# Spectral mixing and FFN in one kernel: loads reordered, scheduler weights replaced, work moved between engines

## The chip, the cores and the metric

The kernel runs on one core of a Trainium2 chip. The metric is device time in microseconds (us), the median of several executions. A core has a TensorE (matmul), a VectorE, a ScalarE, a GpSimd and a SyncE; in the profile they are PE (with PEld for its weight loads), DVE, ACT, POOL and SP. All transfers between DRAM and the core's memory (SBUF) are issued here by SyncE and run on 16 DMA engines. TensorE writes to PSUM, from where VectorE or ScalarE must copy results to SBUF.

## The reference

```python
# x: 1 x 2048 x 512, w_r, w_i: 2048 x 257, w1: 512 x 1792, w2: 1792 x 512, all bf16
def _layernorm(x, axis=-1, eps=1e-5):
    m = jnp.mean(x, axis=axis, keepdims=True)
    v = jnp.var(x, axis=axis, keepdims=True)
    return (x - m) / jnp.sqrt(v + eps)

def _A_ref(x, w_r, w_i):                       # global spectral filter
    X = rfft2(x.astype(float32), axes=(-2, -1))
    X = X * (w_r + 1j * w_i)
    return irfft2(X, s=(S, D), axes=(-2, -1)).astype(bfloat16)

def _B_ref(x, w1, b1, w2, b2):                 # dense FFN with squared ReLU
    h = einsum("bsd,df->bsf", x, w1) + b1
    r = where(h > 0, h, 0)
    return einsum("bsf,fd->bsd", r * r, w2) + b2

h  = x + _A_ref(_layernorm(x), A_w_r, A_w_i)
h2 = h + _B_ref(_layernorm(h), B_w1, B_b1, B_w2, B_b2)
```

## The kernel before

Both transforms are done as matmuls with tables of sines that the kernel computes itself. The 2048 rows lie as 128 partitions x 16 groups g. A forward first level along the rows (tables KR, one per group, scaled by 1/std of the row) is followed by a transform along the columns (GF) and a second level along the rows (EF), in eight pairs `pr` of frequencies. The products with W, their sums and folds follow on VectorE, then the inverse (EI, GI, KI). For a pair other than 0 the mirrored frequency is needed too: it is made either on VectorE ("X<-AB") or by more matmuls (`BY_PE`). Groups 0 and 1 are finished on a short path of their own; the others are finished one by one while the FFN of earlier groups runs on TensorE. The FFN runs in five chunks of 2, 3, 4, 4 and 3 groups.

No engine reorders its own instructions. Their order is fixed when the program is built, by a list scheduler: each `add` names an engine (or several to choose from), an assumed duration, what it reads and writes, a priority and, for transfers, an assumed time to landing (`lag`). The scheduler simulates these and emits each engine's instructions in that order.

```python
    def add(self, eng, w, fn, reads=(), writes=(), prio=0.0, alloc=None, at=0.0, shared=False, lag=0.0,
            uses=(), order=()):
        ways = dict(zip(eng, w)) if isinstance(eng, tuple) else {eng: w}
# ... (cut: choice of the task that can start first, buffers, the lock between DVE and POOL)

    CH = ((0, 2), (2, 4), (4, 8), (8, 12), (12, 16))
    LAND = (3.4, 3.7, 6.0, 6.3, 6.6)
    for c, (a, b) in enumerate(CH):
        add("SP", 0.45, lambda a=a, b=b: sy.dma_start(xs[:, a:b, :], xv[:, a:b, :]),          # L254
            writes=[("x", g) for g in range(a, b)], prio=c, at=0.7, lag=LAND[c])
    for i in range(2):                       # W: natural half, then the mirrored half through DRAM
        add("SP", 0.5, lambda i=i: sy.dma_start(W[i][:, 0:9, :], wv[i][:, 0:9, 1:L + 1]), writes=[("Wn", i)],
            prio=5 + i, lag=9.0)
        add("SP", 0.5, lambda i=i: sy.dma_start(wx[i][:].rearrange("k j l -> j k l"),
                                                wv[i].rearrange("k j l -> j k l")[9:16, ::-1, 1:L + 1]),
            writes=[("wx", i)], prio=7 + i, lag=10.0)
        add("SP", 0.5, lambda i=i: sy.dma_start(W[i][:, 9:16, :], wx[i][:]), reads=[("wx", i)], writes=[("Wr", i)],
            prio=20 + i, lag=4.0)                                                             # L265
# ... (cut: index tables on POOL; KF from kft, the sine of fiK)
    act(1.2, lambda: sc.activation(fiE[0][:], idxE[:], ACT.Identity, scale=cE[:]), 0.3, ...)
    act(1.2, lambda: sc.activation(fiE[1][:], idxE[:], ACT.Identity, scale=cE[:], bias=qtc[:]), 0.4, ...)
    # then Sin of fiE[i] -> EF[:, i], and EF[:, 2] = -EF[:, 0]; EI[:, i] are DMA transposes of EF[:, i]

    ON_ACT = (4, 7, 10, 13)                  # groups whose statistics ScalarE takes
    BATCH = ((0, 2), (2, 4), (4, 8), (8, 12), (12, 14), (14, 16))
        # per batch, on POOL: rs1 = var + eps; rs1 = rs1 ** -0.5
            add(("DVE", "POOL"), (0.2, 0.41), kr, reads=[("rs", bi), "KF"], writes=[("KR", g)], prio=z - 5, shared=True)
        # first level (L391, L393): 8 matmuls of 256 columns for two groups; copies of it to Bt (L399)
    # FFN loads: W1, W2, b1b, b2b
        add("SP", 0.5, lambda d=d, s=s: sy.dma_start(d, s), writes=[("FW", k)], prio=30 + k, lag=15.0, reads=["EF0"])

    BY_PE = (3, 5, 7)
    act(1.07, lambda: sin_of(flat(GI[:]), lo(flat(fiI[:]))), 27.0, reads=["fiI"], writes=["GI0"])
    act(1.4, lambda: sc.activation(junk[:, 0:1], eps[:], ACT.Sqrt), 28.0, reads=["GI0", "eps"], writes=["sqrt"])
    dve(0.15, lambda: ve.tensor_copy(b1f[:], b1b[:]), 200.0, reads=[("FW", 2)], writes=["b1f"], shared=True)
    # pairs pr = 0..7: p2 (L449) -> U (L458) -> p3 (L475-514) -> AB (L521) -> X (L528, not BY_PE)
        for i in range(2):                   # L538; mirrored half Wr for every pair but 0
            k = ("mA", "mB")[i]
            dve(0.61, lambda pr=pr, i=i: prod(pr, i), z, reads=[("X", pr), ("Wn", i)] + [("Wr", i)] * (pr > 0),
                writes=[(k, pr)], alloc=(k, (k, pr)))
    # Z (L546), fold M (L557, L559), p4 (L579), T2 (L588)
            act(0.25, lambda: et(7, 0, 2), z, reads=[("p4", 7)], writes=["T2a"])   # groups 0, 1 need T2a alone
            dve(0.6, lambda: et(7, 9, 16, ve.tensor_copy), z + 3, reads=[("p4", 7)], writes=["T2"])
            act(0.59, lambda: et(7, 2, 9), z + 9, reads=[("p4", 7)], writes=["T2"])
# ... (cut: short path of groups 0 and 1)

    CHUNKS = ((0, 2), (2, 5), (5, 9), (9, 13), (13, 16))
            if c > 0:                        # preparation of group g
                # s5: 4 matmuls (L678-681) -> p5;  od: half of p5 copied by ScalarE (L686)
                # lv1: q = p5 +- od, FP32, 2 on VectorE (L691)
                # spec: 4 columns of R (L700); lv2, k = 0..3: R <- q (L708), 127 columns each:
                    ve.tensor_tensor(o, x, y, (ALU.add, ALU.subtract, ALU.subtract, ALU.add)[k])
                # s6: one matmul of 512 columns, KI x R (L714)
                # hs = p6 + x (L716); square sum of hs - mean on ScalarE (L597)
            pool(1.17, lambda g=g: gp.tensor_tensor(hb[:, g, :], hs[:, g, :], b2b[:], ALU.add), late + 80 + g,
                 reads=[("hs", g), ("FW", 3), ("UT", c)], writes=[("hb", g)])                # L719
        # per chunk: rs2 = sqrt(...), reciprocal; u = (hs + nm1) * rs2 on VectorE for every group (L756);
        # two halves of transposes (L765) for the whole chunk; UT copied by ScalarE and VectorE (L771)
        for f in range(NF):                  # NF = 14
            # up: 4 matmuls of 128 n columns -> ph (L784); relu with bias b1f on ScalarE -> rl (L791)
            # sqr: act = rl * rl on VectorE (L797)
        # down: 14 matmuls of 512 columns per group -> po (L806); ot = po + hb on VectorE (L814); store
```

Of the kernel before, what the change touches and what calls it, by code (L numbers as in the profile page):

```python
# [15 lines left out]
P = 128  # L16
# [17 lines left out]
class Plan:  # L34
# [6 lines left out]
    def __init__(self, caps):  # L41
        self.tasks, self.caps, self.use, self.made = [], caps, {}, {}
        self.free = {e: 0.0 for e in self.HOP}
        self.held = {t: [] for t in caps}
        self.lock = {"DVE": 0.0, "POOL": 0.0}
        self.log = []

    def add(self, eng, w, fn, reads=(), writes=(), prio=0.0, alloc=None, at=0.0, shared=False, lag=0.0,
            uses=(), order=()):
        ways = dict(zip(eng, w)) if isinstance(eng, tuple) else {eng: w}  # L50
        t = dict(eng=None, ways=ways, w=0.0, fn=fn, reads=list(reads), writes=list(writes), prio=prio, alloc=alloc, at=at,
# [36 lines left out]
    def run(self):  # L88
# [7 lines left out]
        while any(left.values()):  # L96
# [28 lines left out]
            if t["alloc"]:  # L125
                tag, key = t["alloc"]
                _, old = self.slot(tag)
                if old is not None:
                    self.held[tag].remove(old)
                self.held[tag].append(key)  # L130
            t["end"] = r + t["w"]
# [8 lines left out]
            t["fn"](*([e] if len(t["ways"]) > 1 else []))  # L140
# [3 lines left out]
def kernel(  # L144
# [42 lines left out]
    rs2 = persist.tile([P, G], FP32, name="rs2")  # L187
    eps = persist.tile([P, 1], FP32, name="eps")
    mv2 = persist.tile([P, 2], FP32, name="mv2")
    junk = persist.tile([P, D], BF16, name="junk")  # L190

# [7 lines left out]
    CN = fwd.tile([P, 3, P], BF16, name="CN")  # L199
# [6 lines left out]
    fz = fwd.tile([P, 512], BF16, name="fz")  # L206
# [23 lines left out]
                 "ph": 3, "po": 2, "pp": 3, "rl": 6, "act": 2, "od": 2, "q": 2, "R": 3, "u2": 2, "UT": 2, "ot": 3})  # L230
    add = plan.add

    def mm_tile(key, dt=FP32):
        T[key] = ps.tile([P, 4096 // mybir.dt.size(dt)], dt, tag="mm", name="m_" + str(key[0]))
        return T[key]
# [16 lines left out]
    LAND = (3.4, 3.7, 6.0, 6.3, 6.6)  # L252
# [6 lines left out]
    for i in range(2):  # L259
        add("SP", 0.5, lambda i=i: sy.dma_start(W[i][:, 0:9, :], wv[i][:, 0:9, 1:L + 1]), writes=[("Wn", i)],  # L260
            prio=5 + i, lag=9.0)
        add("SP", 0.5, lambda i=i: sy.dma_start(wx[i][:].rearrange("k j l -> j k l"),
                                                wv[i].rearrange("k j l -> j k l")[9:16, ::-1, 1:L + 1]),
            writes=[("wx", i)], prio=7 + i, lag=10.0)
# [41 lines left out]
    dve(0.15, lambda: ve.memset(eps[:], EPS), 0.0, writes=["eps"])  # L306
# [10 lines left out]
    for t in range(2):  # L317
        for r in range(2):
            dve(0.34, lambda t=t, r=r: ve.tensor_scalar(fiG[:, t, r, :], idxG[:], pF[:, 3 + t:4 + t],
                                                        float((QT, HT)[r]), ALU.mult, ALU.add),  # L320
                0.6, reads=["pF", "idxG"], writes=[("fiG", t)], shared=True)
    dve(0.33, lambda: ve.scalar_tensor_tensor(
# [4 lines left out]
    act(1.2, lambda: sc.activation(fiE[0][:], idxE[:], ACT.Identity, scale=cE[:]), 0.3, reads=["idxE", "cE"],  # L327
        writes=["fiE0"])
    act(1.2, lambda: sc.activation(fiE[1][:], idxE[:], ACT.Identity, scale=cE[:], bias=qtc[:]), 0.4,
        reads=["idxE", "cE", "qtc"], writes=["fiE1"])  # L330
    act(0.2, lambda: sin_of(flat(kft[:]), lo(fiK[:])), 0.1, reads=["fiK"], writes=["kft"])
    for t in range(2):
        act(0.6, lambda t=t: sin_of(flat(GF[:, t]), lo(flat(fiG[:, t]))), 0.6 + t / 10, reads=[("fiG", t)],
            writes=["GF"])
    for i in range(2):
        act(1.1, lambda i=i: sin_of(flat(EF[:, i]), lo(fiE[i][:])), 0.5 + i / 10, reads=[f"fiE{i}"],
            writes=[f"EF{i}"])
    dve(0.46, lambda: ve.tensor_scalar(EF[:, 2], EF[:, 0], -1.0, None, ALU.mult), 3.0, reads=["EF0"],
# [12 lines left out]
    ON_ACT = (4, 7, 10, 13)  # L351
    BATCH = ((0, 2), (2, 4), (4, 8), (8, 12), (12, 14), (14, 16))
    RT = float(1.0 / np.sqrt(D))
    for bi, (a, b) in enumerate(BATCH):
        z = 10 * bi + 10
        for g in range(a, b):
            if g in ON_ACT:
                act(0.67, lambda g=g: sc.activation(junk[:], xs[:, g, :], ACT.Identity, scale=-RT / D,
                                                    accum_out=nmr[:, g:g + 1]), z - 30, reads=[("x", g)],
                    writes=[("sm", g)])  # L360
                act(0.67, lambda g=g: sc.activation(junk[:], xs[:, g, :], ACT.Square, scale=RT, bias=nmr[:, g:g + 1],
                                                    accum_out=mv1[:, g, 1:2]), z - 30, reads=[("x", g), ("sm", g), "mv1z"],
                    writes=[("mv", g)])
            else:
                def bn(g=g):
# [6 lines left out]
        pool(0.3, lambda a=a, b=b: gp.tensor_scalar(rs1[:, a:b], mv1[:, a:b, 1], EPS, None, ALU.add), z - 1,  # L372
             reads=mvs, writes=[("va", bi)])
        pool(0.4 + 0.16 * (b - a), lambda a=a, b=b: gp.tensor_tensor(rs1[:, a:b], rs1[:, a:b], mhalf[:, 0:b - a],
                                                                   ALU.pow), z - 1, reads=[("va", bi), "mhalf"],
             writes=[("rs", bi)])
        for g in range(a, b):
            def kr(e, g=g):
                (ve if e == "DVE" else gp).tensor_scalar(flat(KR[:, g]), flat(KF[:]), rs1[:, g:g + 1], None, ALU.mult)  # L379
            add(("DVE", "POOL"), (0.2, 0.41), kr, reads=[("rs", bi), "KF"], writes=[("KR", g)], prio=z - 5, shared=True)  # L380
# [37 lines left out]
    BY_PE = (3, 5, 7)  # L418
    dve(0.25, lambda: ve.tensor_scalar(CN[:], EF[:, 1, 3:8:2], -1.0, None, ALU.mult), 75.0, reads=["EF1"],
# [6 lines left out]
    act(1.07, lambda: sin_of(flat(GI[:]), lo(flat(fiI[:]))), 27.0, reads=["fiI"], writes=["GI0"])  # L426
    act(1.4, lambda: sc.activation(junk[:, 0:1], eps[:], ACT.Sqrt), 28.0, reads=["GI0", "eps"], writes=["sqrt"])
    for e in range(2):
        dve(0.3, lambda e=e: ve.tensor_scalar(GI[:, e::2], GI[:, e::2], hsc[:] if e else WSC, None, ALU.mult), 180.0,
# [3 lines left out]
    dve(0.15, lambda: ve.tensor_scalar(nm1[:, ON_ACT[0]::3], nmr[:, ON_ACT[0]::3], 1.0 / RT, None, ALU.mult), 190.0,  # L433
# [6 lines left out]
    for pr in range(8):  # L440
# [18 lines left out]
        if pr < 2:  # L459
            add(("ACT", "DVE"), (0.59, 0.67), lambda e, pr=pr, eu=eu: eu(pr, 0, 1, COPY[e]), reads=[("p2", pr, 0)],  # L460
                writes=[("U", pr), ("U", pr, 0)], uses=[("p2", pr)], alloc=("U", ("U", pr)), prio=z + 2)
            add(("ACT", "DVE"), (0.59, 0.67), lambda e, pr=pr, eu=eu: eu(pr, 1, 2, COPY[e], False),
                reads=[("p2", pr, 1)], order=[("U", pr, 0)], writes=[("U", pr), ("U", pr, 1)], uses=[("p2", pr)],
                prio=z + 2)
        else:
            act(0.93, eu, z + 2, reads=[("p2", pr)], writes=[("U", pr)], alloc=("U", ("U", pr)))
# [124 lines left out]
        else:  # L591
            act(0.25, lambda: et(7, 0, 2), z, reads=[("p4", 7)], writes=["T2a"])
            dve(0.6, lambda: et(7, 9, 16, ve.tensor_copy), z + 3, reads=[("p4", 7)], writes=["T2"])
            act(0.59, lambda: et(7, 2, 9), z + 9, reads=[("p4", 7)], writes=["T2"])
# [62 lines left out]

    CHUNKS = ((0, 2), (2, 5), (5, 9), (9, 13), (13, 16))
# [6 lines left out]
    def per(n, tab_):  # L665
        return tab_[n - 1]

    for c, (a, b) in enumerate(CHUNKS):
# [3 lines left out]
        for g in range(a, b):  # L672
            z = late + g
            if c > 0:
# [7 lines left out]
                add("PE", 0.26, s5, reads=["T2", "T2a", "GI"] + [("UT", 0)] * (g > 2), writes=[("p5", g)], prio=early + 5, alloc=("pp", ("p5", g)))  # L682
# [4 lines left out]
                act(0.37, od, z, reads=[("p5", g), ("UT", 0)], writes=[("od", g)], alloc=("od", ("od", g)))  # L687

                def lv1(g=g, i=0):
                    q = buf(ffn, ("q", g), "q", [P, 2, 2, P], FP32, 2) if i == 0 else T["q", g]  # L690
                    ve.tensor_tensor(q[:, i], T["p5", g][:, 0:256].rearrange("p (a c) -> p a c", a=2),  # L691
                                     T["od", g][:, ::-1, :], (ALU.add, ALU.subtract)[i])
                for i in range(2):
                    dve(0.35, lambda g=g, i=i: lv1(g, i), z, reads=[("p5", g), ("od", g)],
                        order=[("qh", g)] * i,
                        writes=[("q", g), ("qh", g)] if i == 0 else [("q", g)], alloc=("q", ("q", g)) if i == 0 else None)

                def spec(g=g):
                    R = buf(ffn, ("R", g), "R", [P, 512], BF16, 3)
                    ve.tensor_copy(R[:].rearrange("p (a b c) -> p a b c", a=2, b=2)[:, :, ::-1, 0],  # L700
                                   T["q", g][:, :, :, 0])
                dve(0.14, spec, z, reads=[("q", g)], writes=[("R", g), ("Rh", g)], alloc=("R", ("R", g)))

                def lv2(g=g, k=0):
# [145 lines left out]
```

## Time and profile before

| | |
|---|---|
| median of 3 runs | 200.49 us (199.92 to 201.56) |
| span of the profiled execution | 198.2 us, mean granted TensorE clock 0.919 |
| PE busy | 163.4 us, 82% |
| DVE busy | 131.3 us, 66% |
| ACT busy | 108.6 us, 55% |
| POOL busy | 41.7 us, 21% |
| DMA, all queues | 12.13 MB, of it 5 to 9 tenths of the engines busy in the first 40 us |

In the profile "L708" is line 708 of the kernel before. Durations are those of single instructions unless a count (x4) stands behind; neighbouring instructions of an engine may overlap by some tens of nanoseconds. A matmul's own duration contains its pipeline, so for the pace of many of them the distance between starts is taken. The granted clock is the share of full speed that TensorE was given.

### The profile page before, as it was taken

The page shows a single profiled execution, that of the slowest core. Times are in us where ns is not written, and L with a number is a line of the kernel's source. Part 1 is how long each engine was busy: PE and PEld are TensorE (multiplying, and loading weights), DVE is VectorE, ACT ScalarE, POOL GpSimd, SP SyncE. Part 2 cuts the span into 40 slices and gives each one's busy share as a digit, 9 for nine tenths or more (in the row PEclk, how much of TensorE's full clock was granted, in tenths as well). Part 3 has the DMA queues.
Part 4 walks back from the last instruction along what each step waited for, and adds up shares of the span by engine and source line. Part 5 has one row for each costly group of instructions (what it writes and reads, how often), then busy time and mean ns, then how long its engine had stood idle before and what let it go on. Part 6 is the DMA issues. An engine that isn't in the chain of part 4 may idle for free.

```text
span 198.2 us, 2693 instructions
## 1 busy us (share of the span) xinstructions
PE 163.4 (82%) x932; PEld 90.7 (46%) x932; DVE 131.3 (66%) x344; ACT 108.6 (55%) x187; POOL 41.7 (21%) x64
## 2 busy tenths in 40 slices
PE   7545865599983758999399897998999999999992
PEld 2223543376761426853265453453454444456540
DVE  5496261659999366899999999999722543135321
ACT  6996673199884143873378723778410772029500
POOL 7389760000000022132343204203200000000000
PEclk9978589699999585899879999999999999999998
DMA  5978999600000000000000000100010000110001
GB/s 132 371 254 191 353 252 238 206 0 0 5 0 0 0 0 2 3 0 28 26 0 3 0 26 26 31 2 0 0 53 30 26 0 0 53 49 8 0 29 50
DMA packets 15595, 12.13 MB, mean 61 GB/s; under 512 B 6110, under 2 KB 14174, under 8 KB 15582
## 3 DMA queue, kind: packets, MB, share of 16 engines
q1 hardware_dynamic: 15582, 11.97, 19.9%
q8 instruction: 7, 0.11, 0.3%
q14 instruction: 6, 0.05, 0.1%
HBM read 8.92 MB, written 3.01 MB: 60 GB/s over the span
## 4 chain that ended last, share of the span: by engine, by line
PE 39%; DVE 20%; ACT 1%; POOL 1%; issue 0%; DVEq 0%
PE po L806 20%; PE ph L784 16%; DVE act L797 5%; DVE R L708 5%; DVE hs L716 3%; DVE q L691 2%; DVE ot L814 1%; ACT rl L791 1%; PE pp L765 1%; DVE u L732 1%; PE pp L714 1%; POOL hb L719 1%; DVE R L700 1%; DVE UT L771 1%; DVE u L756 1%
## 5 line engine op out<-in xcount | busy, mean ns | idle before, releaser
L791 ACT ACTIVATE rl<-ph,b1f 128x384 bf16<-128x384 f32 (+2 forms) x70 | 41.3, 601 | 30.2 <-PE ph L784 29.0
L784 PE MATMUL ph<-UT,W 128*128 128x384 bf16 (+2 forms) x280 | 53.7, 347 | 0.0
L806 PE MATMUL po<-W,act 128*128 128x512 bf16 x224 | 50.7, 379 | 0.0
L719 POOL TENSOR_TENSOR hb<-hs,b2b 128x512 f32<-128x512 bf16 x16 | 20.2, 1267 | 93.4 <-DVE hs L716 48.2
L797 DVE TENSOR_TENSOR act<-rl 128x384 bf16<-128x384 bf16 (+2 forms) x70 | 30.6, 441 | 13.0 <-ACT rl L791 12.6
L784 PEld LDWEIGHTS <-W 128*128 128x128 bf16 x280 | 28.2, 102 | 21.0 <-issue 0.3
L806 PEld LDWEIGHTS <-act 128*128 128x128 bf16 x224 | 21.6, 98 | 26.2 <-issue 1.9
L814 DVE TENSOR_TENSOR ot<-po,hb 128x512 bf16<-128x512 f32 x16 | 11.0, 689 | 20.9 <-PE po L806 20.7
L391 PE MATMUL m_p<-KR,xs 128*128 128x256 bf16 x32 | 11.2, 360 | 8.4 <-POOL KR L379 7.9
L708 DVE TENSOR_TENSOR R<-q 128x127 bf16<-128x127 f32 x56 | 16.9, 339 | 0.0
L597 ACT ACTIVATE junk<-hs,nm 128x512 bf16<-128x512 bf16 x14 | 10.0, 717 | 8.2 <-DVE hs L716 8.2
L449 PE MATMUL m_p<-GF,Bt 128*128 128x256 bf16 x64 | 9.2, 299 | 4.8 <-DVE U L458 3.4
L458 ACT CAST U<-m_p 128x1024 bf16<-128x1024 f32 (+1 forms) x8 | 8.9, 1174 | 6.7 <-PE m_p L449 4.8
L579 PE MATMUL m_p<-EI,M 128*128 128x256 bf16 x56 | 8.6, 294 | 3.8 <-DVE M L557 3.7
L393 PE MATMUL m_p<-KR,xs 128*128 128x256 bf16 x32 | 11.2, 364 | 0.0
L588 ACT CAST T<-m_p 128x1024 bf16<-128x1024 f32 (+2 forms) x9 | 7.9, 886 | 6.0 <-DVE T L588 3.2
L691 DVE TENSOR_TENSOR q<-pp,od 128x256 f32<-128x256 f32 x28 | 10.6, 409 | 0.0
L449 PEld LDWEIGHTS <-Bt 128*128 128x128 bf16 x64 | 6.6, 106 | 6.7 <-issue 3.6
L379 POOL TENSOR_SCALAR KR<-KF,rs 128x256 bf16<-128x256 bf16 x10 | 9.4, 952 | 0.6
L716 DVE TENSOR_TENSOR hs<-pp,xs 128x512 bf16<-128x512 f32 x14 | 9.5, 679 | 0.0
L686 ACT COPY od<-pp 128x256 f32<-128x256 f32 x14 | 5.2, 369 | 7.7 <-DVE q L691 5.2
L399 ACT CAST Bt<-m_p 128x1024 bf16<-128x1024 f32 (+1 forms) x7 | 6.2, 887 | 5.2 <-PE m_p L393 3.7
(162 smaller groups left out, 210.9 us busy)
## 6 DMA issues: line engine op xcount, KB each, us to landing
W<-in_B_w_dram SPq DMA_DIRECT2D x2, 1792.0 KB, 8.4
out_dram<-ot SPq DMA_DIRECT2D x16, 128.0 KB, 1.8
xs<-in_A_x_dram SPq DMA_DIRECT2D x3, 512.0 KB, 6.5
W<-wx SPq DMA_DIRECT2D x2, 448.0 KB, 4.4
W<-in_A_w_r_dram SPq DMA_DIRECT2D x1, 576.0 KB
W<-in_A_w_i_dram SPq DMA_DIRECT2D x1, 576.0 KB, 6.4
xs<-in_A_x_dram SPq DMA_DIRECT2D x2, 256.0 KB, 5.8
wx<-in_A_w_r_dram SPq DMA_DIRECT2D x1, 448.0 KB
```

Of the source, the lines that this page charges most:

```text
L391: mm(o, lhsT=xs[:, g, P * t:P * t + P], rhs=KR[:, g, 0].unsqueeze(1).to_broadcast([P, 2, P]), start=True, stop=False)
L393: mm(o, lhsT=xs[:, g, 256 + P * t:256 + P * t + P], rhs=KR[:, g], start=False, stop=True)
L449: mm(puv[:, q, e, :], lhsT=Bt[:, 2 * t + 1 - e, 2 * pr + q, :], rhs=gfv[:, t, :, e, :], start=(t == 0), stop=(t == 1))
L691: ve.tensor_tensor(q[:, i], T["p5", g][:, 0:256].rearrange("p (a c) -> p a c", a=2), T["od", g][:, ::-1, :], (ALU.add, ALU.subtract)[i])
L708: ve.tensor_tensor(o, x, y, (ALU.add, ALU.subtract, ALU.subtract, ALU.add)[k])
L716: dve(0.67, lambda g=g: ve.tensor_tensor(hs[:, g, :], T["p6", g][:], xs[:, g, :], ALU.add), z, reads=[("p6", g)], writes=[("hs", g)])
L719: pool(1.17, lambda g=g: gp.tensor_tensor(hb[:, g, :], hs[:, g, :], b2b[:], ALU.add), late + 80 + g, reads=[("hs", g), ("FW", 3), ("UT", c ...
L784: mm(p[:, 0:P * n], lhsT=W1[:, d, bass.ts(f, P)], rhs=T["UT", c][:, d, 0:P * n], start=(d == 0), stop=(d == ND - 1))
L791: sc.activation(r[:, 0:P * n], T["ph", c, f][:, 0:P * n], ACT.Relu, bias=b1f[:, f:f + 1], scale=1.0)
L797: ve.tensor_tensor(t[:, f, 0:P * n], r[:, 0:P * n], r[:, 0:P * n], ALU.mult)
L806: mm(p[:], lhsT=T["act", c][:, f, bass.ts(i, P)], rhs=W2[:, f, :], start=(f == 0), stop=(f == NF - 1))
L814: ve.tensor_tensor(o[:], T["po", g][:], hb[:, g, :], ALU.add)
```

## The change

Five things are bundled. (1) x is issued ahead of W, a dummy Sin loads the sine table at once, and one argument table moves to POOL. (2) The scheduler's assumed durations and landing times are replaced by ones read from a trace; matmuls on zeros are put into gaps of TensorE that the scheduler foresees; which groups ScalarE takes, the batches, and the pairs done `BY_PE` change. (3) hb, the addition of the second bias, moves from GpSimd to VectorE. (4) The preparation of groups for the FFN is spread: group i of chunk c may start after the matmuls for f = 2i of chunk c-1; chunks 1 and 2 are normalised and transposed group by group, on either engine. (5) For groups 2 to 8 the second column level, four additions and a copy on VectorE, is done by nine matmuls that accumulate in PSUM.

```diff
+            self.gap = r - self.free[e]
+    def warm(p):
+        for _ in range(min(24, int((plan.gap - 0.2) / 0.08))):
+            mm(p[:, 0:P], lhsT=fz[:, 0:P], rhs=fz[:, 0:P], start=True, stop=True)
     def mm_tile(key, dt=FP32):
+        warm(T[key])
-    LAND = (3.4, 3.7, 6.0, 6.3, 6.6)
+    LAND = (3.2, 3.4, 4.2, 4.8, 5.6)
@@ natural half of W, mirrored half to DRAM
-            prio=5 + i, lag=9.0)
+            prio=5 + i, at=1.0, lag=7.0)
-            writes=[("wx", i)], prio=7 + i, lag=10.0)
+            writes=[("wx", i)], prio=7 + i, at=1.0, lag=8.0)
+    act(1.5, lambda: sc.activation(junk[:, 0:1], eps[:], ACT.Sin), -100.0, reads=["eps"], writes=["sinset"])
-    act(1.2, lambda: sc.activation(fiE[1][:], idxE[:], ACT.Identity, scale=cE[:], bias=qtc[:]), 0.4,
+    pool(1.9, lambda: gp.tensor_scalar(fiE[1][:], idxE[:], cE[:], float(QT), ALU.mult, ALU.add), 1.9,
-    ... EF[:, 2] = -EF[:, 0] ... 3.0, reads=["EF0"],
+    ... EF[:, 2] = -EF[:, 0] ... 79.0, reads=["EF0"],
-    ON_ACT = (4, 7, 10, 13)
-    BATCH = ((0, 2), (2, 4), (4, 8), (8, 12), (12, 14), (14, 16))
+    ON_ACT = (5, 7, 9, 11)
+    SQ = 6
+    BATCH = ((0, 4), (4, 8), (8, 12), (12, 14), (14, 16))
-        pool(0.3, ... rs1 = var + eps
+        dve(0.13, ... rs1 = var + eps
-            add(("DVE", "POOL"), (0.2, 0.41), kr, ...
+            add(("DVE", "ACT"), (0.28, 0.43), kr, ...
-    BY_PE = (3, 5, 7)
+    BY_PE = (4, 5, 6, 7)
-    act(1.07, ... GI ..., 27.0, reads=["fiI"], writes=["GI0"])
-    act(1.4, ... ACT.Sqrt), 28.0, reads=["GI0", "eps"], writes=["sqrt"])
+    act(1.07, ... GI ..., 27.0, reads=["fiI", ("KR", 13)], writes=["GI0"])
+    act(1.4, ... ACT.Sqrt), 0.0, reads=["GI0", "eps", ("p4", SQ)], writes=["sqrt"])
+            act(0.32, lambda: et(7, 0, 2), z, reads=[("p4", 7)], writes=["T2a"])
+            add(("ACT", "DVE"), (0.5, 0.55), lambda e: et(7, 2, 8, COPY[e]), prio=z + 30, reads=[("p4", 7)], order=["T2a"], writes=["T2"])
+            add(("ACT", "DVE"), (0.58, 0.62), lambda e: et(7, 8, 16, COPY[e]), prio=z + 60, reads=[("p4", 7)], order=["T2a"], writes=["T2"])
@@ FFN
+    def gate(c, i, n):
+        return [("ph", c - 1, 2 * i)] if c > 1 else []
+    BY_PE2 = (2, 3, 4, 5, 6, 7, 8)
+    ONE = (1, 2)
-                add("PE", 0.26, s5, reads=["T2", "T2a", "GI"] + [("UT", 0)] * (g > 2), ...
+                add("PE", 0.26, s5, reads=["T2", "T2a", "GI"] + gate(c, g - a, n), ...
@@ s6 of groups in BY_PE2 (q is bf16 there)
+                    for k in range(4):
+                        o = p[:, 128 * k + 1:128 * k + 128]
+                        for b in range(2):
+                            v = q[:, k // 2, b, :0:-1] if k % 2 == 0 else q[:, k // 2, b, 1:]
+                            mm(o, lhsT=KI[:, 1 if b == 1 and k in (1, 2) else 0], rhs=v, start=(k == 0 and b == 0), stop=False)
+                    mm(p[:].rearrange("p (a b c) -> p a b c", a=2, b=2)[:, :, ::-1, 0], lhsT=KI[:, 0], rhs=q[:, :, :, 0],
+                       start=False, stop=True)
-            pool(1.17, ... hb ..., late + 80 + g, reads=[("hs", g), ("FW", 3), ("UT", c)], ...
+            dve(0.62, ... hb ..., late + 180 + g, reads=[("hs", g), ("FW", 3), ("ph", c, 4)], writes=[("hb", g)], shared=True)
@@ chunks 1 and 2 by group (ONE): sqrt, reciprocal, nr2 = nm1 * rs2, un on DVE or ACT, transposes, UT on ACT or DVE
+                dve(0.16, ... ve.tensor_tensor(nr2[:, p0:p1], nm1[:, p0:p1], rs2[:, p0:p1], ALU.mult), z, ...
+                add(("DVE", "ACT"), (0.42, 0.72), un, ...
+            parts = [(g - a, g - a + 1, 0, 4) for g in range(a, b)] if c in ONE else [(0, n, 0, 2), (0, n, 2, 4)]
@@ relu: on DVE too in chunk 0
+            add(("ACT", "DVE") if c == 0 else ("ACT",), (0.28 + 0.085 * n, 0.1 + 0.14 * n)[:2 if c == 0 else 1], relu, prio=z, ...
```

Cut from the diff: most replaced durations, names and buffer counts. Lines with "..." are shortened.

## The prediction

> **What bounds the kernel now.** I read the chain of waits first, then busy time by stage, then the order of time of the queues at the seams. The chain, in order of time, reaches back only to 73.5 us, but its last third is plain:
>
> ```profile
> 152.21 12.09 PE ph L784 x56
> 164.29 12.09 PE po L806 x56
> 176.38 9.10 PE ph L784 x56
> 185.48 9.08 PE po L806 x42
> 194.56 0.04 DVEq L814
> ```
>
> From 139 us TensorE runs without a hole: 56 matmuls of 512 columns in 12.09 us are 0.216 us each, 56 of 384 columns 0.1625 us each. Nothing is to be had there but fewer matmuls. The busy time of stretches that I cut at the seams (engine columns PE, PEld, DVE, ACT, POOL; then the granted clock):
>
> ```profile
> 42.50:65.00 22.50, 17.57 (x135) 12.49 (x132) 21.43 (x48) 17.79 (x18) 0.00 (x0) 0.97 0.00 1
> 65.00:77.20 12.20, 7.91 (x44) 4.79 (x44) 6.21 (x14) 4.04 (x11) 2.31 (x2) 0.64 0.00 1
> 77.20:99.30 22.10, 18.10 (x125) 11.45 (x123) 20.17 (x65) 11.71 (x29) 5.44 (x4) 0.89 0.04 13
> 99.30:120.60 21.30, 20.48 (x129) 11.37 (x128) 21.18 (x62) 13.19 (x29) 5.42 (x4) 0.96 0.03 11
> 120.60:139.40 18.80, 16.73 (x95) 8.03 (x93) 18.29 (x48) 14.31 (x28) 5.77 (x5) 1.00 0.04 11
> 139.40:194.60 55.20, 55.15 (x279) 26.51 (x276) 20.89 (x46) 19.91 (x33) 1.27 (x1) 1.00 0.07 24
> ```
>
> From 42.5 to 65 (the spectral products) VectorE is 95% busy, and so it is from 77 to 139 (FFN while the next token groups are prepared), where TensorE has its holes. Before 42.5 neither is the bound. The timeline there (SyncE issues transfers; the bracket is the idle time before an instruction and what ended it):
>
> ```profile
> 1.89 4.01 SPq L254 DMA_DIRECT2D xs<-in_A_x_dram  x5
> ...
> 8.30 0.69 DVE L367 BATCH_NORM_STATS2 st<-xs 128x6 f32<-128x512 bf16 x1 [0.89 <-DMA xs<-in_A_x_dram]
> ...
> 27.14 6.61 SPq L416 DMA_DIRECT2D b2b<-in_B_b_dram  x1
> 33.80 1.90 SPq L265 DMA_DIRECT2D W<-wx  x2
> ...
> 35.91 0.17 DVE L435 CAST b1f<-b1b 128x14 f32<-128x14 bf16 x1 [3.98 <-DMA b1b<-in_B_b_dram]
> ...
> 42.53 0.69 DVE L538 TENSOR_TENSOR mA<-X,W 128x1024 bf16<-128x1024 bf16 x1
> ```
>
> Two limits lie on top of each other. The first level (L391, L393) starts at 12.5 and ends at 28.7, because x lands late and GpSimd makes most of the scaled KR tables (ten of 0.95 us). Behind it stands the load of the mirrored half of W, issued last: 33.80 plus 4.4 us to landing gives 38.2, the second 39.7. Every product from pair 1 on needs it (42.53 is the first). The DMA engines show 9, 7, 8, 9, 9, 9, 6 tenths from 5 to 40 us: moving everything there costs about 33 us of the first 40.
>
> **What the Trainium skill says.** "DMA: Bandwidth & Descriptors", section "Issuing engines are not separate DMA queues": transfers all end on the same 16 DMA engines. So reordering loads changes who waits, not the sum; the tenths above agree. "SBUF — State Buffer", section "SBUF: two separate sides": the port pair shared by VectorE and GpSimd is an exclusive lock for a whole instruction. The trace agrees: L708 takes 0.28 us elsewhere and 1.24 us at 103.14, beside GpSimd's hb of 1.20 us at 103.03. "ScalarE: Activation LUTs", section "What ACT_TABLE_LOAD costs": about 1283 ns; the trace has three at 1283 ns, and after the one for Sin none before Identity and Square. "TensorE: Matmul & The Clock Gate", Part 1: the clock is halved after idleness; the 0.64 from 65 to 77.2 is that.
>
> **The change, part by part.**
>
> *Start.* x is issued at 0.7 instead of 1.89, and no longer behind 1.1 MB of W (some 4 us at the 254 GB/s of the first 10 us), so I expect statistics at about 4.5 to 5, not 8.3. A dummy Sin pulls the table load from 5.37 to about 1 and saves the Identity load; one argument table goes to GpSimd. KF is then there at about 4.6 instead of 7.4. KR leaves GpSimd for VectorE (0.33) or ScalarE (about 0.45). VectorE then has 12 statistics of 0.85 with their aggregate and some 12 KR, 14 us: the first level ends near 20, not 28.7. The Sqrt load (28.06 to 29.34, in front of the last Bt copy) moves into ScalarE's idle time near 61.
>
> That is 9 us at the front, but I do not count it: pair 1's products still need the mirrored W, behind x, W, W1, W2 and both biases. By the diff the loads of W1 and W2 still depend only on EF and the mirrored W on its round trip through DRAM. What improves is that no transposes of EF stand between W1 and W2 (SyncE spent 7.22 us there) and the holes at 10 to 20 us close. Bounds: 39.7 if nothing closes; 2 + 32 = 34 if all do. I choose 37.
>
> *Products.* Before, pair 1's products start at 42.53 and pair 7 ends at 64.96: 22.4 us, that is seven pairs of 2.86 (two products 1.33, sums 0.76, folds 0.77) and three butterflies X of 0.78. In the new kernel pairs 4 to 7 combine on TensorE (L498 form), and pairs 1 and 2 have theirs done while W is awaited, since X has two buffers; pair 3's stays: 7 x 2.86 + 0.78 = 20.8. TensorE has 0.85 us more in all here and stays below VectorE. With 0.3 from landing to start and 0.7 of friction: 37 + 20.8 + 1.0 = 58.8.
>
> *The seam to the FFN* took 12.2 (64.96 to 77.2). Warm-up matmuls in planned gaps should keep the clock: pair 7's last transform ran at 0.42 per 256-column matmul instead of 0.27 and lasted 2.0 (-1.0), the transforms after it -0.6. The piece of T2 that groups 0 and 1 need is copied first, not behind VectorE's 0.62 (-0.4). Group 1's normalisation took 1.06 against 0.4 for its kind, locked out by hb (-0.65). 12.2 - 2.65 = 9.5; the FFN starts at 68.3.
>
> *FFN.* It takes 194.56 - 77.2 = 117.4. TensorE's floor: up 6.1 + 2 x 9.1 + 2 x 12.1 = 48.5 (256 columns by proportion), down 224 x 0.216 = 48.4, spectral 14 x (0.23 + 0.22) = 6.3, transposes 56 x 0.056 = 3.1, together 106.3. So 11.1 is lost, all before 139. The windows give it: idle 4.0 + 0.8 + 2.1, and slow clock 0.11 x 18.1 + 0.04 x 20.5 = 2.8; the rest is inside the groups.
> VectorE in those 62 us loses: four L708 and one L700 for groups 2 to 8, 7 x (4 x 0.20 + 0.09) = 6.2; the GpSimd lock, which I estimate at 11 us from the excess of the means (L708 56 x 0.06, L797 about 6, L700 and u the rest). It gains: hb at 0.66, sixteen times, 10.6, of which only the first five or so are needed before 117 and the others fit after 139 (20.9 busy of 55); small nr2 operations, 1; some relu of chunk 0. Net about -12 of 60. Also chunks 1 and 2 go group by group, and preparation of chunk c waits for single ph of chunk c-1, so chunk 2's no longer competes with chunk 1's, whose UT came only at 98.4.
> TensorE pays for the second level: 9 small matmuls of 127 columns, 0.50, instead of one of 0.22: 7 x 0.28 = 2.0.
> I leave a loss of 2.0 until chunk 1 and 1.5 after: 106.3 + 2.0 + 3.5 = 111.8, that is 5.6 better.
>
> *Sum.* 68.3 + 111.8 = 180.1, plus 3.6 from last matmul to end as now = 183.7 of span; the median lies 2.3 above the profiled span now (200.49 - 198.2): 186.0.
>
> **Rivals.**
> *The mirrored W does not come earlier.* For it: it is still last in the queue, and the DMA engines are already near full. Against it: 7, 8 and 6 tenths leave some 4 us. Then 39.7 instead of 37: 188.7. If x in front also delays its round trip, 43 and 192.
> *VectorE only swaps one load for another in the FFN*: hb on it costs 10.6, the lock 11. If the plan puts hb and nr2 into the busy stretch, only the 2.0 of TensorE is left: 186.0 + 5.6 + 2.0 = 193.6. Against it: hb has the lowest priority of its chunk.
> *TensorE becomes the bound earlier* by warm-ups that are not free: up to 24 of about 0.06 are 1.4 us each time a planned gap is none in truth, and the stall for W is not a planned gap, so the clock is halved after it. Two such places and 2 us of slow clock: 190.
> *The loads pack tightly* (34): 183.
>
> **Range and chances.** Start and FFN are two gains of different cause, about 8.9 and 5.6; each alone is over the 4 us that are 2%. The load could miss by 5, the FFN by 5, rarely together: 179.5 to 193. Faster by over 2% means under 196.5: 0.92. Within 2%: 0.06. Slower: 0.02, for an order in the plan that blocks a queue.
>
> **What would show it.** Right: first statistics at about 5; first level over by about 20; then TensorE and VectorE idle until a wait that DMA ends near 37; fold of pair 7 ends near 59; up-matmuls from about 68; no L708-like operation over 1 us; UT of chunk 1 about 14 us after the FFN starts, not 21; TensorE without holes from there. Wrong: W landing after 39 or not being waited for at all (then the front's 9 us count, and I am too slow by several us); hb bunched where TensorE waits; a FFN of 117.

## The result and the profile after

The changed kernel takes 188.72 us (187.39 to 189.42), 0.940 of before (95% interval 0.933 to 0.947). The prediction was 186.0, range 179.5 to 193. So the sum was close, but its terms missed in opposite directions: the FFN starts 6.1 us later than predicted (74.43 for 68.3) and is 4.5 us shorter (107.3 for 111.8).

First the page's chain of what ended last, after the change, by engine and by line:

```profile
PE 61%; DMA 13%; DVE 11%; ACT 8%; issue 3%; SPq 2%; DVEq 0%; ACTq 0%
PE ph L828 26%; PE po L854 26%; DMA b1b<-in_B_b_dram 7%; DMA EI<-EF 4%; DMA xs<-in_A_x_dram 3%; PE pp L726 2%; DVE Z L561 2%; ACT Bt L413 2%; PE pp L808 2%; DVE mA L553 2%; DVE mB L553 2%; ACT junk L369 2%; ACT junk L372 1%; DVE M L572 1%; DVE M L574 1%
```

The chain before (PE 39%, DVE 20%) reached back only to 73.5 us and says nothing of the transfers; this one reaches to the start. Two late transfers stand in it: the load of b1, a tensor of 3.5 KB, with 7%, and the transposed EF with 4%. The mirrored half of W, on which the prediction had built, is not there. Busy time by stage, cut at the new seams (PE, PEld, DVE, ACT, POOL; then the granted clock, the busy share of the DMA engines and GB/s):

```profile
24.00:33.60 9.60, 4.14 (x31) 2.98 (x32) 1.54 (x6) 1.32 (x2) 0.00 (x0) 0.86 1.01 295
33.60:38.40 4.80, 3.09 (x10) 1.41 (x10) 4.20 (x10) 2.80 (x3) 0.00 (x0) 0.57 1.03 243
38.40:62.93 24.53, 21.64 (x191) 16.47 (x192) 20.77 (x46) 19.66 (x20) 0.00 (x0) 1.00 0.07 15
62.93:74.43 11.50, 7.53 (x68) 5.70 (x68) 6.91 (x17) 4.51 (x12) 0.00 (x0) 0.89 0.01 1
74.43:181.74 107.31, 106.51 (x647) 58.03 (x656) 75.33 (x211) 60.88 (x124) 0.00 (x0) 1.00 0.06 19
```

From 24 to 33.6 TensorE's matmuls are busy 4.14 of 9.60 us and VectorE and ScalarE under 1.6, while the DMA engines are full, as they are until 38.4. In the FFN TensorE is busy 106.51 of 107.31 us at full clock; before it was 110.45 of 117.40 with clock 0.97. Even of the 0.80 most is no hole: 12 matmuls are missing in this trace (it has 276 of 280 up and 216 of 224 down), and e1 and e2, which have them all, show 0.13 of idle time. The timelines of SyncE, VectorE and, last, TensorE show what holds the front:

```profile
0.72 2.29 SPq L263 DMA_DIRECT2D xs<-in_A_x_dram  x5
...
5.07 1.27 DVE L378 BATCH_NORM_STATS2 st<-xs 128x6 f32<-128x512 bf16 x2
...
19.42 1.12 SPq L430 DMA_DIRECT2D W<-in_B_w_dram  x2
20.59 4.80 SPq L430 DMA_DIRECT2D b1b<-in_B_b_dram  x1
25.43 5.89 SPq L430 DMA_DIRECT2D b2b<-in_B_b_dram  x1
31.36 0.91 SPq L274 DMA_DIRECT2D W<-wx  x2
32.36 5.85 SPq L422 DMA_TRANSPOSE EI<-EF  x2
```

```profile
33.56 0.17 DVE L450 CAST b1f<-b1b 128x14 f32<-128x14 bf16 x1 [6.99 <-DMA b1b<-in_B_b_dram]
...
38.40 0.69 DVE L553 TENSOR_TENSOR mA<-X,W 128x1024 bf16<-128x1024 bf16 x1
...
47.73 0.76 DVE L543 TENSOR_TENSOR X<-AB 128x512 bf16<-128x512 bf16 x2 [2.78 <-ACT AB L536]
...
62.51 0.42 DVE L574 TENSOR_TENSOR M<-Z 128x512 bf16<-128x512 bf16 x1
```

```profile
35.09 0.59 PE L527 MATMUL m_p<-U,EF 128*128 128x512 bf16 x1 [6.40 <-DVE U L473]
...
40.29 0.22 PE L589 MATMUL m_p<-EI,Z 128*128 128x128 bf16 x1 [0.75 <-DMA EI<-EF]
```

Statistics start at 5.07 (8.30 before), and the second transform (L464) at 23.95 (30.12 before). Then VectorE stands 6.99 us for b1, which the FFN needs only at 75. Products of pair 1 start at 38.40 (42.53 before), the fold of pair 7 (the last M<-Z) ends at 62.93 (64.96), the first up matmul (the FFN's first product, into ph) runs at 74.43 (77.2). The stretch between these two is called the seam, and X<-AB of a pair its butterfly. So of some 6 us won in the first 24, less than 3 are left when the FFN starts. The FFN itself gives the other ten: 117.4 before, 107.3 after.

### The profile page after: what moved, and what is told of

Its sections match the earlier page's. It is cut to its first block, busy times and chain, and to the rows that moved or that the text cites. A ratio compares the mean times of both kernels' runs of the same rounds, so it can differ in the third digit from the quotient of the medians.

```text
span 185.3 us, 2990 instructions
## 1 busy us (share of the span) xinstructions
PE 162.3 (88%) x1105; PEld 98.5 (53%) x1120; DVE 127.1 (69%) x351; ACT 108.8 (59%) x195; POOL 11.6 (6%) x32
## 4 chain that ended last, share of the span: by engine, by line
PE 61%; DMA 13%; DVE 11%; ACT 8%; issue 3%; SPq 2%; DVEq 0%; ACTq 0%
PE ph L828 26%; PE po L854 26%; DMA b1b<-in_B_b_dram 7%; DMA EI<-EF 4%; DMA xs<-in_A_x_dram 3%; PE pp L726 2%; DVE Z L561 2%; ACT Bt L413 2%; PE pp L808 2%; DVE mA L553 2%; DVE mB L553 2%; ACT junk L369 2%; ACT junk L372 1%; DVE M L572 1%; DVE M L574 1%
## 5 line engine op out<-in xcount | busy, mean ns | idle before, releaser
L836 ACT ACTIVATE rl<-ph,b1f 128x384 bf16<-128x384 f32 (+2 forms) x62 | 37.4, 616 | 28.8 <-PE ph L828 26.9
L828 PEld LDWEIGHTS <-W 128*128 128x128 bf16 x280 | 26.8, 99 | 19.6 <-issue 0.3
L845 DVE TENSOR_TENSOR act<-rl 128x384 bf16<-128x384 bf16 (+2 forms) x70 | 25.2, 368 | 8.7 <-ACT rl L836 7.8
L750 DVE TENSOR_TENSOR hb<-hs,b2b 128x512 f32<-128x512 bf16 x16 | 10.7, 684 | 0.0
L405 PE MATMUL m_p<-KR,xs 128*128 128x256 bf16 x32 | 7.3, 272 | 2.5 <-ACT KR L393 1.4
L536 ACT CAST AB<-m_p 128x1024 bf16<-128x1024 f32 x7 | 7.2, 1032 | 3.6 <-PE m_p L529 1.4
L464 PE MATMUL m_p<-GF,Bt 128*128 128x256 bf16 x64 | 8.4, 282 | 0.8 <-DVE Bt L413 0.8
L239 PEld LDWEIGHTS <-fz 128*128 128x128 bf16 x124 | 8.3, 103 | 1.6 <-DVE pI L319 1.2
L378 DVE BATCH_NORM_STATS2 st<-xs 128x6 f32<-128x512 bf16 x12 | 7.9, 662 | 0.0
L816 ACT COPY UT<-pp 128x512 bf16<-128x512 bf16 (+2 forms) x6 | 4.1, 687 | 6.2 <-PE pp L808 6.2
L464 PEld LDWEIGHTS <-Bt 128*128 128x128 bf16 x64 | 6.3, 101 | 2.5 <-DVE Bt L413 1.0
L795 ACT ACTIVATE u<-hs,nr,rs 128x512 bf16<-128x512 bf16 x7 | 5.4, 808 | 3.5 <-DVE nr L787 3.5
L407 PE MATMUL m_p<-KR,xs 128*128 128x256 bf16 x32 | 7.3, 272 | 0.0
```

What stands on the lines that cost most here:

```text
L239: mm(p[:, 0:P], lhsT=fz[:, 0:P], rhs=fz[:, 0:P], start=True, stop=True)
L464: mm(puv[:, q, e, :], lhsT=Bt[:, 2 * t + 1 - e, 2 * pr + q, :], rhs=gfv[:, t, :, e, :], start=(t == 0), stop=(t == 1))
L750: dve(0.62, lambda g=g: ve.tensor_tensor(hb[:, g, :], hs[:, g, :], b2b[:], ALU.add), late + 180 + g, reads=[("hs", g), ("FW", 3), ("ph", c ...
L828: mm(p[:, 0:P * n], lhsT=W1[:, d, bass.ts(f, P)], rhs=T["UT", c][:, d, 0:P * n], start=(d == 0), stop=(d == ND - 1))
L836: sc.activation(r[:, 0:P * n], T["ph", c, f][:, 0:P * n], ACT.Relu, bias=b1f[:, f:f + 1], scale=1.0)
L845: ve.tensor_tensor(t[:, f, 0:P * n], r[:, 0:P * n], r[:, 0:P * n], ALU.mult)
```

## The experiments

A name stands for a kernel; each is the changed kernel with the edit shown, if nothing else is said. Times are medians with lowest and highest; a ratio is to the kernel before. Runs e1 to e4 are from one chip, e5 to e11 and after_again from another, and two series of the changed kernel gave 188.72 and 188.48.

### What holds the front: b1, the mirrored W, or EF

The theory after reading the trace (A): the FFN loads stand in the queue ahead of two things that the products need, the mirrored half of W and the last transposes of EF. The wait for b1 only covers them.

**e1_b1f_late**

```diff
-    ... b1f[:], b1b[:]), 200.0, reads=[("FW", 2)], ...
+    ... b1f[:], b1b[:]), 200.0, reads=[("FW", 2), "T2a"], ...
```

> The changed kernel with the cast of b1 (b1f, which waits 7.0 us on VectorE for the b1 load) moved behind the last copy of T2a; nothing else in any engine's order changes. Theory A, two late transfers stand one behind the other: the 7.0 us wait is gone, but TensorE then stands at the first inverse transform until the transposed EF lands at about 40 us, as it does now, so the FFN starts at 73.5 to 74.5 instead of 74.4 and the time falls by 0 to 1 us (187.5 to 189, ratio to before about 0.94). Theory B, the b1 wait alone holds the front: the whole rest moves up by 5 to 7 us, 182 to 184, ratio about 0.91. Theory C, the mirrored half of W holds it: first products of pair 1 at about 36.5 instead of 38.4 and the time falls by about 2 us.

Measured: 189.94 (189.54 to 190.23), so no gain at all. The 7 us wait was real, and behind it stood the two others (timelines of TensorE and VectorE in e1_b1f_late):

```profile
39.87 0.27 PE L588 MATMUL m_p<-EI,Z 128*128 128x128 bf16 x1 [8.93 <-DMA EI<-EF]
```

```profile
37.57 0.69 DVE L553 TENSOR_TENSOR mA<-X,W 128x1024 bf16<-128x1024 bf16 x1 [6.04 <-DMA W<-wx]
...
49.43 0.76 DVE L543 TENSOR_TENSOR X<-AB 128x512 bf16<-128x512 bf16 x2 [4.92 <-ACT AB L536]
```

Now VectorE stands 6.04 us for the mirrored W and TensorE 8.93 us for EF. Theory B falls. The FFN starts at 76.40, not at 73.5 to 74.5 as theory A had it: TensorE runs at half clock until 44.9 (37.8 in the changed kernel), 24 matmuls of 256 columns take 4.05 us from 42.35 against 2.78, and pair 3's butterfly comes at 49.43 instead of 47.73. That this follows from the edit is not shown: e5 and e7, which leave b1's cast where it was, take 3.84 and 3.93 us for the same 24.

**e2_ffn_loads_last**: as e1, and

```diff
-    ... writes=[("FW", k)], prio=30 + k, lag=15.0, reads=["EF0"])
+    ... writes=[("FW", k)], prio=30 + k, lag=15.0, reads=["EF0", ("Wr", 0), ("Wr", 1), ("EI", 0), ("EI", 1), ("EI", 2)])
```

> As e1_b1f_late, and the four FFN loads (W1, W2, b1, b2) issued behind the mirrored half of W and the transposes of EF; the order of the other engines stays that of e1. Theory A: the first level still ends near 23, products of pair 1 start near 30 instead of 38.4, the fold of pair 7 ends at 52.5 to 56 instead of 62.9, the FFN starts at 64 to 67 and the time is 178 to 182, ratio about 0.90. Theory B (the b1 wait alone): the same as e1. Theory D, the loads of W1 and W2 are then too late for the FFN: TensorE waits for them at the first up matmul and the gain is under 3 us.

Measured: 178.98 (178.40 to 179.74), 11 us under e1 on the same chip and about ten under the changed kernel. TensorE, VectorE, ScalarE and GpSimd run the same instructions in the same order as in e1; only SyncE's order differs. SyncE and VectorE in its timeline:

```profile
19.41 1.00 SPq L274 DMA_DIRECT2D W<-wx  x2
20.50 5.02 SPq L422 DMA_TRANSPOSE EI<-EF  x2
25.57 1.16 SPq L430 DMA_DIRECT2D W<-in_B_w_dram  x2
```

```profile
31.49 0.69 DVE L553 TENSOR_TENSOR mA<-X,W 128x1024 bf16<-128x1024 bf16 x1
...
53.08 0.42 DVE L574 TENSOR_TENSOR M<-Z 128x512 bf16<-128x512 bf16 x1
```

Neither product nor transform waits for a transfer, the fold of pair 7 ends at 53.50, the first up matmul runs at 65.2. The theory D (W1 and W2 too late) falls too: no up matmul waits for them. The loads put last without b1's cast put late were not run; b1 lands 14.2 us after its issue at 26.78 here, so VectorE would have stood for it until about 41 (an estimate from these two numbers).

Which of the two transfers is it? Two complements, each with b1f late.

**e11_W_only**: FFN loads behind the mirrored W, not behind EF (`reads=["EF0", ("Wr", 0), ("Wr", 1)]`); the negative of EF stays last.

> The complement: the mirrored half of W goes ahead of the FFN loads, the last transposed part of EF (its negative) stays behind them; b1f late; every other order is that of e2. Theory A: products of pair 1 start at 31 to 32 as in e2, but TensorE stands at pair 0's inverse transform until EF lands at 37 to 41, pair 3's butterfly waits for it, and the FFN starts at 72 to 76: time 186.5 to 190. Rival, the mirrored W is the one that counts: time within 2 us of e2, 179 to 181.

Measured: 189.47, ratio 0.944 (0.937 to 0.951). Products of pair 1 start at 32.09, and all is lost again at EF (TensorE's timeline):

```profile
40.17 0.26 PE L589 MATMUL m_p<-EI,Z 128*128 128x128 bf16 x1 [8.66 <-DMA EI<-EF]
```

**e10_EI_only**: FFN loads behind EF (`reads=["EF0", ("EI", 0), ("EI", 1), ("EI", 2)]`), the mirrored W behind them (`order=[("FW", 3)]`).

> Of the two transfers that e2 moved, the transposes of EF alone go ahead of the FFN loads; the mirrored half of W stays last (the scheduler also puts one butterfly and a few copies earlier); b1f late. Theory A: TensorE does not stand for EF, VectorE stands for the mirrored W, which lands at 38 to 44 (SyncE waits for EF's last part before it issues W1); from the first product of pair 1 to the end of pair 7's fold it takes 20.5 to 21.5 us, the sum that the prediction made, instead of 24.5; time 185 to 191. Rival, EF alone holds the front: 180 to 182.

Measured: 191.11, ratio 0.951 (0.946 to 0.957). VectorE's timeline:

```profile
45.22 0.69 DVE L553 TENSOR_TENSOR mA<-X,W 128x1024 bf16<-128x1024 bf16 x1 [11.98 <-DMA W<-wx]
...
66.08 0.42 DVE L574 TENSOR_TENSOR M<-Z 128x512 bf16<-128x512 bf16 x1
```

It waits 11.98 us for W, which lands at 45.13, later than the expected 38 to 44, and then needs 21.28 us (45.22 to 66.50) for the products, in the expected 20.5 to 21.5. So each transfer alone holds the front: the FFN starts at 75.8 with EF late, at 78.2 with W late and at 76.4 with both (e1), and at 65.2 only when both are early. That is 10 to 11 us for the pair, nothing for either one.

**e3_b1_runs**: the 2-byte elements of b1.

```diff
-    (b1b[:], B_b1.rearrange("(i p) -> p i", p=P)),
+    (b1b[:], B_b1.rearrange("(p i) -> p i", p=P)),
```

The biases then stand at other places than the reference's; the work is the same.

> The changed kernel with b1 loaded as 128 runs of 28 bytes instead of 1792 of 2 bytes (the bias then stands at the wrong places, the work is the same); orders unchanged. If the 2-byte elements themselves take DMA time: the b1 wait on VectorE falls from 7.0 to about 4 us, all that is queued behind (b2, mirrored W, transposes of EF) lands 2 to 4 us earlier, and the time falls by 2 to 3 us to about 186. If only the place behind W1 and W2 counts: wait 6.5 to 7, time unchanged within 0.5 us.

Measured: 185.72 (185.17 to 185.73), 3 us under the median of the changed kernel. By the profiles, which have the same mean clock (0.970), it is 1.6 us: 183.7 against 185.3. SyncE and VectorE:

```profile
25.61 0.98 SPq L430 DMA_DIRECT2D b2b<-in_B_b_dram  x1
26.64 0.91 SPq L274 DMA_DIRECT2D W<-wx  x2
```

```profile
32.45 0.17 DVE L450 CAST b1f<-b1b 128x14 f32<-128x14 bf16 x1 [5.95 <-DMA b1b<-in_B_b_dram]
```

The issue of b2 takes 0.98 us instead of 5.89, the mirrored W is issued at 26.64 instead of 31.36. The wait for b1 itself shrinks by 1 us only, not by the 3 expected: most of it is the place behind W1 and W2. EF, behind b1, lands 3.1 us earlier (37.19 for 40.25). But of the 1.6 us by which the FFN starts earlier (72.85), 1.1 are b1's own, since products of pair 1 start at 37.29, and only 0.5 come from EF, through pair 3's butterfly (wait 2.28 for 2.78).

**e4_before_x_first**: the kernel before, with the loads of W held back (`at=1.0`) so that x goes first.

> The kernel before with x issued ahead of W and nothing else (the scheduler then moves a few copies of the first level too). Theory A: statistics start at about 5.5 to 7 instead of 8.3, the first level ends 1 to 3 us earlier than 28.7, but the products of pair 1 still start at 41.5 to 43, and the time is 199 to 201.5, ratio 0.99 to 1.00. Rival, the start of the statistics sets the front: 3 us less, 197.5, ratio 0.985.

Measured: 203.82 (202.77 to 205.52) beside 201.59 (197.26 to 202.41) for the kernel before on the same chip. Six of those seven executions lie 1.9% or more above the seventh (197.26), so no ratio is given; but the fastest of this kernel lies above all seven: no gain. Statistics start only at 7.33, because VectorE stands for KF (6.93, the sine table), the second transform starts as before (29.99 for 30.12), and the wait for b1 grows to 8.77, until 38.08 instead of 35.91. Products of pair 1 start at 46.02, not at the expected 41.5 to 43. Reordering x alone brings forward nothing that the products wait for.

### What shortened the FFN

**e6_lv2_dve**: `BY_PE2 = ()`.

> The changed kernel with the second column level of groups 2 to 8 back on VectorE (one matmul of 512 columns instead of nine small ones). Theory A, VectorE is short only until chunk 1 is ready: TensorE has 2.0 us less to do, VectorE 6.2 us more in 70 to 105; chunk 1's first up matmul comes 1 to 3 us later than 14.0 us after the FFN's start and TensorE waits for it; time 189 to 191. Rival, TensorE is the only bound of the FFN now: FFN length falls from 107.3 to 105.5 to 106.5, time 187 to 188.

Measured: 190.61, ratio 0.956 (0.947 to 0.966). The FFN takes 111.3 us (73.8 to 185.1) although TensorE has less to do (2.0 in all by the prediction's count). Chunk 1's first up matmul comes 16.8 us after the FFN's start, and TensorE's timeline has its holes back, at chunk 1 and chunk 2:

```profile
90.64 0.81 PE L828 MATMUL ph<-UT,W 128*128 128x384 bf16 x4 [0.67 <-ACT UT L816]
...
109.71 0.40 PE L808 MATMUL pp<-ident,u 128*128 128x128 bf16 x4 [1.28 <-DVE u L793]
110.78 1.02 PE L828 MATMUL ph<-UT,W 128*128 128x512 bf16 x4 [0.67 <-ACT UT L816]
```

So moving the second level is worth up to 4 us of FFN, net of its price on TensorE. The holes are 2.6 us. Of the rest about 2 (an estimate) are granted clock: it is half for the first 5.2 us of the FFN here and for 0.9 in the changed kernel, and whether the edit causes that is not shown.

**e5_hb_pool**: hb on GpSimd again, `pool(1.17, ... gp.tensor_tensor ..., late + 180 + g, ...)`.

> The changed kernel with hb back on GpSimd (same priority and same gate as in the change). Theory A, the lock was the larger part of VectorE's load in the FFN, but VectorE now has room (in 80 to 110 us it is busy 22.6 of 30): VectorE operations over 1 us come back, 10 or more of them, TensorE gets holes of 0.5 to 3 us in the FFN, whose length rises from 107.3 to 108 to 110, time 189 to 192. Rival, the move of hb was only a swap of one load for another: FFN length 107 to 107.5 and time unchanged within 0.5 us.

Measured: 190.39, ratio 0.953 (0.946 to 0.961). FFN 108.2 us. Only one operation of VectorE in it is over 1 us (a square of 1.37 at 127.44), not ten. But the lock is there: 11 operations take 0.3 to 1.0 us longer than others of their kind, 6.4 us together (12 and 9.6 us in the kernel before). Its one visible cost is at the seam, which takes 12.3 us (TensorE's timeline):

```profile
73.17 1.23 PE L770 MATMUL pp<-ident,u 128*128 128x128 bf16 x8 [2.24 <-POOL hb L750]
```

The same wait is 1.68 in the changed kernel. Kernels that share the changed FFN have lengths of 107.3 to 108.4: 107.3 to 107.4 with a mean clock of 0.996 (after, after_again, e3), 108.1 to 108.4 with 0.986 to 0.988 (e1, e2, e8, e10, e11). So no cost of the lock in the FFN is shown, and the ratios' intervals overlap.

**e7_no_spread**:

```diff
-    ... reads=["T2", "T2a", "GI"] + gate(c, g - a, n), ...
+    ... reads=["T2", "T2a", "GI"] + [("UT", 0)] * (g > 2), ...
-    ONE = (1, 2)
+    ONE = ()
```

> The changed kernel with the gate of the preparation as before and with chunks 1 and 2 prepared as wholes. Theory A, the spread and the work group by group are what closed TensorE's holes before chunk 1: chunk 1's first up matmul comes at 17 to 20 us after the FFN's start instead of 14.0, FFN length 110 to 113, time 191 to 194. Rival, VectorE's relief (hb, second level) did it and the spread adds nothing: FFN length 107 to 108.5, time within 1 us of 188.7.

Measured: 186.17, ratio 0.934 (0.927 to 0.940). FFN 107.5: the rival is right, spread and work by group together add nothing (each alone was not run). Chunk 1's first up matmul comes 16.1 us after the FFN's start, and TensorE has no hole before it. From the fold's end to the first up matmul it even takes 10.1 us instead of 11.5: the changed kernel's gate leaves chunk 1 free, so the products of three groups take the three PSUM buffers "pp", and the transposes of group 0 wait 1.68 us, until VectorE has copied the first group out (71.50; they start at 71.61). Here one group stands ahead, and they wait 0.50.

**e8_no_warm**: no matmuls on zeros in mm_tile.

> The changed kernel without the matmuls on zeros in foreseen gaps (the 20 long ones at the start stay). Theory A: first level at half clock as before and over about 1 to 2 us later, which costs nothing since VectorE waits for b1 until 33.6; the last inverse transforms and the seam at half clock: time from the fold of pair 7 to the first up matmul 12.5 to 14 instead of 11.5; total 190 to 192. Rival, they do not matter or stand in the way: 187.5 to 189.

Measured: 190.56, ratio 0.953 (0.946 to 0.960), about 2 us over the changed kernel (188.72 and 188.48), with overlapping intervals of the ratios. The seam takes 11.7 us against 11.5, and the last inverse transform 1.28 for eight matmuls against 1.27. So the seam is not where they act. In the first level, where the clock is 0.87 instead of 1.00 (10 to 23 us), nothing is lost: the second transform starts at 24.06 instead of 23.95. The profile's span is 3.5 us longer: 1.1 is a b1 that landed later (TensorE resumes at 36.22 instead of 35.09), 1.2 more come from there to the fold of pair 7 (between 40 and 65 us the clock is 0.89 instead of 1.00), and 0.9 in the FFN. But e5 and e7, which have the matmuls on zeros, show a clock of 0.92 and 0.91 there and lose 0.9 and 1.1 us in the same stretch. An effect of these matmuls on the time is therefore not shown.

### The two together

**e9_last_no_spread**: e2 and e7 in one.

> The version that should beat both: FFN loads last and b1f late (as e2_ffn_loads_last), and the preparation not spread (as e7_no_spread). If the two add up: seam from the fold of pair 7 to the first up matmul 10.2 as in e7 instead of 11.7, FFN 107.5 to 108.5, time 176.5 to 178.5. If the spread was worth something: 179 to 181.

Measured: 177.34 (176.75 to 178.69), ratio 0.884 (0.880 to 0.889), under both kernels; it leaves nothing of the computation out. The fold of pair 7 ends at 53.65, the first up matmul runs at 63.76, and the FFN is 107.6 long. It stands beside 188.48 for the changed kernel in the next run, on the same chip.

**after_again**

> The changed kernel once more, as it stands, beside the three others on one chip: 187.5 to 189.5, ratio 0.935 to 0.945; it shows how far single profiles differ (start of the FFN 74 to 76, length 107 to 108.5).

Measured: 188.48 (187.06 to 190.47), ratio 0.936 (0.930 to 0.942), FFN from 74.3, 107.4 long.

## Why the prediction came out as it did

*Start.* Right. Statistics at 5.07 ("4.5 to 5"), KF at 4.68 to 5.15 (4.6), first level over at 22.5 ("near 20": 2.5 late, ScalarE having the copies and its own statistics to do), and "That is 9 us at the front, but I do not count it" holds.

*The mirrored W at 37.* The time was right, the path was not, and this is the step that failed in kind. "pair 1's products still need the mirrored W" is true, and in e1, where b1 is out of the way, they start at 37.57 for the 37.3 predicted. But in the changed kernel that wait is hidden: VectorE's order puts b1's cast first, and it stands there until 33.56. Products start at 38.40; that two different waits end within 1 us of each other is luck. The prediction had the path wrong for the kernel before already. The line of b1 lay in its own fence (3.98 us, at 35.91), and it did not ask what comes right behind it on VectorE. That is a copy of U (35.99), for which TensorE waits, and then comes ScalarE's AB (TensorE and VectorE, before):

```profile
36.76 2.72 PE L449 MATMUL m_p<-GF,Bt 128*128 128x256 bf16 x12 [3.42 <-DVE U L458]
```

```profile
41.73 0.76 DVE L528 TENSOR_TENSOR X<-AB 128x512 bf16<-128x512 bf16 x2 [2.33 <-ACT AB L521]
```

Pair 1's products at 42.53 waited for this, not for the mirrored W, whose second half had landed at 39.7.

*Products 20.8.* Took 24.53. The term is right as a rate: 7 x 2.86 = 20.0, and e10 gives 21.28 where only W is missing. But "pairs 1 and 2 have theirs done while W is awaited" could not be, VectorE being stuck at b1: two butterflies (41.20 and 47.73) fall inside, 1.56. And 2.78 are the wait for pair 3's AB: TensorE stood for b1's sake (6.40 at 35.09), then for EF until 40.29. That EF would land last, behind W1, W2 and b1, was in the diff ("3.0" to "79.0", and EF's sine on ScalarE behind the statistics) and the prediction took it for a gain ("no transposes of EF stand between W1 and W2"). TensorE's transform for pair 3 stands behind both in its order.

*Seam 9.5.* Took 11.50. Group 1's normalisation took 0.41 as predicted, and T2a is first. The last transform did run at 0.27 per matmul, but e8 shows the same without warm-ups, after the same idle time as before (1.59 us); the clock there is granted in full in both, and half in the kernel before. Not foreseen were the wait for a "pp" buffer, whose end the trace puts down to nothing ("issue"), and two second levels on TensorE ahead of the first up matmul (72.66 to 74.43, 1.77 at half clock).

```profile
71.61 0.38 PE L770 MATMUL pp<-ident,u 128*128 128x128 bf16 x4 [1.68 <-issue]
```

*FFN 111.8.* Took 107.3. The floor, 106.3 + 2.0, less what TensorE did before the first up matmul (two second levels and three spectral groups, at the prediction's rates 2 x 0.50 + 3 x 0.23 = 1.7), is 106.6; so the lost part is 0.7, not the 3.5 allowed. About 0.4 of it is half clock for the first 0.9 us, 0.13 idle. Of the reasons given, the second level carries up to 4.0 (e6), the lock nothing that shows in the FFN (e5), the spread nothing (e7). The prediction's 11 us of VectorE time for the lock was a fair size (9.6 in 12 operations), but blocked time of VectorE is not time of the FFN: in e5 6.4 of it are back, and the FFN is no longer for it. So 6 of the 10.1 us have no single cause here. The lock and the second level both load VectorE, and taking back one while the other stays away can hide what the pair is worth; both together were not taken back. Nor was ScalarE's share of u, VectorE's share of relu, or the new order as such tested.

*Sum.* Errors: +1.1 start of products, +3.0 products (24.53 for 20.8 and 0.7), +2.0 seam, -4.5 FFN, together +1.6 in the span (185.3 for 183.7), and the median lies 3.4 above it, not 2.3, 1.3 of it because the profiled execution (187.39) is the fastest of the four. Of the rivals, the first was nearest in kind: something that W1 and W2 stand in front of comes too late. Its number, 188.7, is met by luck, since it had the mirrored W at 39.7 and the gain in the FFN at 5.6.

## What to carry to other kernels

Ask of every transfer when its data is first used, and let the queue follow that; loads for a stage 40 us ahead stood here before two that the next stage needed, and cost about 10 us (e2 against e1, 11; e9 against e7, 8.8). When a wait ends last, look at what stands behind it in all queues before removing it: here three waits ended within 7 us of each other, and removing one, or clearing two of the three, gained nothing. An instruction that waits for a load and whose result is needed only much later should not be placed in an engine's order ahead of work that is needed now, whatever the scheduler believed about the landing.

## What was not expected

- A load of 3.5 KB in 2-byte elements holds up what is queued behind it: as 128 runs of 28 bytes, the next issue takes 0.98 us instead of 5.89, and the kernel gains 1.6 us by the profiles, 3 by the medians (e3).
- Issuing x before W in the kernel before makes it no faster, 203.82 beside 201.59; the b1 it waits for lands at 38.08 instead of 35.91 (e4).
- With VectorE relieved, putting hb back on GpSimd blocks VectorE for 6.4 us in all, and the FFN stays within the 107.3 to 108.4 us of the others (e5).
- One and the same front comes out in two ways: at half clock until about 38 us (after, after_again, e6) or until about 44 (e5, e7), and then the fold of pair 7 ends about 1 us later. Differences of that size between single profiles need more than one profile.
